# Four moves in the second half of a hand-ordered attention-and-MLP block

## The chip, the cores and the metric

One NeuronCore of a Trainium2 chip runs one program. The metric is its time on the device in microseconds (us), as the median of several executions. Five engines work side by side, each through its own queue in program order: TensorE (PE, matrix products), VectorE (DVE), ScalarE (ACT), GpSimd (POOL), and SyncE (SP), which here issues the transfers.

## The reference

The input x has 2048 rows of 576 numbers. Two branches are added to it: sliding-window attention on the layer-normed x, and a dense MLP with the Mish activation on the same layer-normed x.

```python
xn = _layernorm(x)
# A: 32 heads of 18; each position looks at itself and 7 earlier ones, 2 apart
qkv = xn @ wqkv
logits = einsum("bhsd,bhswd->bhsw", q, kg) * scale      # w = 8 window places
o = einsum("bhsw,bhswd->bhsd", softmax(logits), vg)
A = o @ wo                                              # 576 x 576
# B: 576 -> 4608 -> 576
h = xn @ w1 + b1
B = (h * tanh(softplus(h))) @ w2
return x + A + B
```

All of it is in 32-bit floats.

## The kernel before, in words

**Numbers.** Every matrix operand is kept as two tiles, a *high part* (the value rounded to the format that TensorE reads, written by ACT) and a *low part* (value minus high part, written by DVE or POOL). A product is three matmuls per 128 rows of depth: high x high, high x low, low x high. So `prod`, which multiplies two such rows of depth, issues six matmuls (L669), and `rest`, for the last 64 columns of the 576, two (L675).

**Halves, pairs, parts.** The 2048 rows are done in two halves (`hf` 0 and 1) of 1024. In each half the 4608 hidden columns are done in 18 *pairs* `q` of 2 x 128. For one pair, `m1_part` computes the first MLP product by a scheme with seven products in place of eight, on sums of quarter blocks (`S1`... from `Ss`, and the weight sums `t0`, `t1`), in six *parts*. They use three PSUM banks of the tag "h" (`cur[1]` to `cur[3]`): part 0 fills bank 1 and bank 2, part 2 goes on in bank 1, part 1 fills bank 3 ("the third product"), part 3 goes on in bank 1, part 4 in bank 3 and part 5 in bank 1. After parts 0, 2 and 3, `take` (L703, ACT) copies bank 1 to a tile (c11, c21, c22) before the next part goes on in the same bank. `mish` then adds a bank to such a copy (L714, DVE) and applies Mish (L715, ACT). For the first pair (q = 0) the six parts run in the order 0, 2, 1, 3, 5, 4, and two of the Mish steps are held back until part 5.

**Items.** In the second half the second MLP product of the first eight pairs is also done with seven products instead of eight. Two pairs make a group `e` (0 to 3), with seven *items* `k` (0 to 6), called item e.k here: `p_item` multiplies a left operand (24 matmuls into four "out" banks, L859) and adds the four results to accumulators (`accP`, DVE L865; for some of the first group copied by ACT, L863). Left operands are an activation quarter or a sum: `u_sum` (L801) makes the sums S1 to S4 in place, `u_high` (L807, ACT) the high part, `u_low` (L813, DVE or POOL) the low part, all for each of the group's two pairs `qq`. Items need S3, A22, A11, S1, A12, S2, S4 in this order; the sum S2 is made near item 0. `p_join` (L868, POOL) adds accumulators to each other at the end. Pairs 8 to 17 go the plain way: `m2_cols`, four *chunks* of 24 matmuls each (L880), added up by DVE (L883); `a_split` (L821 ACT, L822 POOL) makes the high and low parts of pair 8's activations, `mish` itself those of the later pairs (L720, L721).

**Attention.** `attention(hf)` is a generator, advanced one *step* at a time. A step first flushes the reduction of the step before (DVE, L538 or L577) and then puts two multiplications on POOL (L533 `pr` or L571 `pv`). Steps of the second half run in the slots listed in `cuts[1]`.

**Order.** All work stands in a list `plan` of *slots*. A slot has its own matmuls (with the evictions behind them) and a list of background functions, filled by `before(i, fn)`, which are issued ahead of the slot's own work. What a slot leaves behind (`pend`, `soon`) is issued in the next slot, around its background. A manual dependency holds each engine to this order, so an operation that waits holds up all behind it on its engine. Around the end of the items the slots are, in order: part 8.4, item 3.3, part 8.5, item 3.4, item 3.5, part 9.0, item 3.6, part 9.1, part 9.2, chunk (1,0), part 9.3, chunk (1,1), part 9.4, chunk (0,0), part 9.5, chunk (0,1), with part q.n for part n of pair q and the chunks being those of pair 8. In the slots from part 9.0 to part 9.1, POOL has in the background: two joins and a low half of `a_split`; two joins and two low halves, and then the low half of a Mish; two joins and a low half.

**The end.** After pair 17's four chunks (1,0), (1,1), (0,0), (0,1) come sixteen output products with `wo` in three parts each (`wo_part`, L1063, in "h" banks). Each needs its attention tile split and summed by `o_split`, in four steps 0 to 3 (DVE L914 and L917; L929 and L930; L935; L938 and L939). For the first output tile these steps use three "h" banks and run beside pair 17's chunks.

Of the kernel before, what the change touches and what calls it, by code (L numbers as in the profile page):

```python
# [17 lines left out]
P = 128  # L18
# [13 lines left out]
OC = 4  # L32
# [7 lines left out]
def block_kernel(ctx: ExitStack, tc: tile.TileContext, x, wq, wo, w1, b1, w2, mask, out):  # L40
    nc = tc.nc
# [617 lines left out]
    cur = {}  # L659
    late = []  # L660

    def bank(hf, q, n):
        cur[n] = ps.tile([P, TB], F32, tag="h", bufs=4, name=f"h{n}_{hf}_{q}")
        return cur[n]

    def prod(ph, wt, off, X, hi, lo, first, last):
        seq = [(off + k, wl, xs + k) for k in range(2) for wl, xs in ((0, hi), (0, lo), (1, hi))]
        for i, (wk, wl, xs) in enumerate(seq):
            nc.tensor.matmul(ph, wt[:, wl, wk * P:(wk + 1) * P], X[:, xs, :],  # L669
                             start=first and i == 0, stop=last and i == len(seq) - 1,  # L670
                             skip_group_check=True)

    def rest(ph, wt, off, X, xs):
        for wl in range(2):
# [52 lines left out]
    def m1_part(hf, q, part):  # L727
        X0, X1 = XTs[hf, 0], XTs[hf, 1]
        if part == 5 and late:
            for fn in late[::-1]:  # L730
                fn()
            late.clear()
        wa, wc, t0, t1 = (done.get((k, hf, q)) for k in ("wa", "wc", "t0", "t1"))
        if part == 0:
            prod(bank(hf, q, 1), wa, 0, X0, 0, 5, True, True)
            take(hf, q, "c11")
            prod(bank(hf, q, 2), wa, 2, X0, 2, 7, True, False)
            rest(cur[2], wa, 4, X0, 4)
            mish(hf, q, 0, 0, cur[2], cur["c11"])
        elif part == 1:  # L740
            prod(bank(hf, q, 3), t1, 0, X1, 0, 5, True, True)
        elif part == 2:
            prod(cur[1], t0, 2, Ss[hf, 1], 0, 2, False, True)
            take(hf, q, "c21")
        elif part == 3:
            prod(cur[1], t0, 0, Ss[hf, 0], 0, 2, False, False)
            rest(cur[1], wc, 2, X1, 4)
            take(hf, q, "c22")
        elif part == 4:
            prod(cur[3], t1, 2, X1, 2, 7, False, False)  # L750
            rest(cur[3], wa, 4, X1, 4)
            mish(hf, q, 1, 0, cur[3], cur["c21"])
        else:
            prod(cur[1], wc, 0, Ss[hf, 2], 0, 2, False, False)
            rest(cur[1], wc, 2, X1, 9)
            mish(hf, q, 0, 1, cur[1])
        if part == 3:
            mish(hf, q, 1, 1, cur[3], cur["c22"])
# [383 lines left out]
    plan = []  # L1142
    at = {}
    US = {"q": 2.75, "z": 2.5, "p": 3.15, "t": 0.6, "o": 2.6}
    PART = (3.2, 1.4, 1.4, 1.8, 1.8, 1.8)

    def add(tag, *fns, alias=None):
        at[tag] = at[alias] = len(plan)
# [2 lines left out]
    def before(i, fn):  # L1151
        plan[max(i, 0)][1].append(fn)

    def qi(hf, g, b, jj, alias=None):
        add(("q", hf, g, b, jj), lambda: qkv_item(hf, g, b, jj), alias=alias)

    def zi(jj, part):
        add(("z", jj, part), lambda: z_part(1, jj, part))

    def mi(hf, q, part, alias=None):  # L1160
        add(("m", hf, q, part), lambda: m1_part(hf, q, part), alias=alias)
# [68 lines left out]
    def quad(hf, q):  # L1230
        if q == 0:
            for part, ids in ((0, (0,)), (2, (1, 2)), (1, (3, 4)), (3, (5, 6)), (5, (7, 8)), (4, (9,))):
                for p_ in {}.get(part, ()) if hf else ():
                    zi(JB - 1, p_)
                if part == 5 and hf == 0:
                    qi(hf, NQ - 1, 0, JB - 1)
                mi(hf, 0, part)
                for i in ids:
                    at["s", hf, 0, i] = len(plan) - 1
            return  # L1240
        if hf and q <= 2 * OC + 1:
            C9 = list(((1,0),(1,1),(0,0),(0,1)))
            if q == 1:
                seq = ((0, (0,)), (2, (1, 2)), (1, (3, 4)), (3, (5, 6)), (4, (7, 8)), (5, (9,)))
            elif q == 2 * OC:
                seq = ((0, (0,)), (1, (1,)), ("N", (2,)), (2, (3,)), ("N", (4,)), (3, (5,)), ("N", (6,)), (4, (7,)), ("N", (8,)),
                                (5, (9,)), ("N", ()))
            elif q == 2 * OC + 1:
                seq = (("N", (0,)), (0, ()), ("N", (1,)), (1, ()), (2, (2,)), ("C", (3,)), (3, (4,)), ("C", (5,)), (4, (6,)), ("C", (7,)), (5, (8,)), ("C", (9,)))
            elif q % 2 == 0:  # L1250
                seq = (0, 1, "N", 2, "N", 3, "N", 4, "N", 5) if q > 2 else (0, 2, "N", 1, "N", 3, "N", 4, "N", 5)
                seq = [(p_, (i,)) for i, p_ in enumerate(seq)]
            else:
                seq = [(p_, (i, 9)[0:1 + (i == 8)]) for i, p_ in enumerate((0, 1, 2, "N", 3, "N", 4, "N", 5))]
            for part, ids in seq:
                if part == "N":
                    pi()
                elif part == "C":
                    pr_(1, q - 1, *C9.pop(0))
                else:  # L1260
                    for p_ in {4:(3,)}.get(part, ()) if q == 1 else ():
                        zi(JB - 1, p_)
                    mi(1, q, part)
                for i in ids:
                    at["s", 1, q, i] = len(plan) - 1
            return
        k = 0
        late_chunks = q == 1 or (hf, q) == (1, NP - 1)
        for i, part in enumerate((0, 1, 2, None, 3, None, 4, None, 5, None) if late_chunks else
                                 (0, 1, None, 2, None, 3, None, 4, None, 5)):  # L1270
            if (hf, q) == (0, NP - 1) and i in (5, 7, 9):
                tr(0, (i - 5) // 2)
            alias = ("s", hf, q, i)
            if part is not None:
                mi(hf, q, part, alias)
            else:
                pr_(hf, q - 1, *CHUNKS[k], alias)
                k += 1
# [65 lines left out]
    for q in range(NP):  # L1344
        if q == 0:
            i = at["q", 0, 3, 1, 0]
            ps_ = dict(raw=i - 3, sums=i - 1, wa=i, wc=i + 1, t0=i + 2, t1=i + 4)
        elif q == 1:
            i = at["q", 0, 3, 0, 0]
# [16 lines left out]
    for q in range(1, 2 * OC + 1):  # L1366
        i = spot(0, q, (3,2)[q > 1])
# [5 lines left out]
    i = spot(0, NP - 1, 0)  # L1373
# [5 lines left out]
    i = at["q", 1, 0, 1, 1]  # L1379
# [4 lines left out]
    i = spot(0, 9, 4)  # L1384
# [10 lines left out]
    for q in range(NP):  # L1395
        if q == 0:
            i = at["z", JB - 1, 0]
            ps_ = dict(wa=i - 7, t0=i - 6, t1=i - 5, wc=i - 4)
        elif q == 1:
            i = spot(1, 0, 0)  # L1400
# [9 lines left out]
    for g, (e, k, s) in enumerate(items):  # L1410
        lead = items[g - 3][2] if g >= 3 else spot(1, 0, 5) + 2 * g
        before(lead + 1, lambda e=e, k=k: p_fetch(e, k))
        for qq in range(2):
            ds = {(0, 0): (-6, -5, -5), (0, 1): (-2, -1, 0), (1, 0): (0, -4, -2), (1, 1): (0, -2, -2), (2, 0): (0, -3, -2), (2, 1): (0, -3, -2), (3, 0): (-4, -3, -2), (3, 1): (-4, -2, -1), (4, 0): (0, -3, -3), (4, 1): (0, -3, -2), (5, 0): (-1, -3, -3), (5, 1): (0, -3, -2), (6, 0): (-4, -3, -1), (6, 1): (-4, -3, -2)}[k, qq]
            for d, f in zip(ds[1:], (u_high, u_low)):
                before(s + d, lambda f=f, e=e, k=k, qq=qq: f(e, k, qq))
            s2 = items[7 * e + (0 if k == 5 else k)][2] + ds[0]
            before(s2, lambda e=e, k=k, qq=qq: u_sum(e, k, qq))
    J = 2 * OC + 1
    for n, (a, b) in enumerate((("P6", "P1"), ("P7", "P6"), ("P6", "P5"), ("P2", "P1"), ("P3", "P6"), ("P4", "P7"), ("P5", "P7"))):  # L1420
        for pr in range(2):
            i = items[-2][2] + 1 + (0,1,2)[n] if n < 3 else at["p", 1, J + 0 - 1, n > 4, pr] + (1, 7, 1, 2)[n - 3]
# [6 lines left out]
    i = at["q", 0, 1, 1, 0]  # L1429
# [3 lines left out]
    i = at["q", 0, 3, 1, 0]  # L1433
# [5 lines left out]
    i = at["q", 1, 0, 1, 1]  # L1439
    for n in range(8):  # L1440
        c, k = divmod(n, 4)
# [7 lines left out]
    for n in range(0, JB, 2):  # L1449
        i = at["q", 0, 1, 0, n]  # L1450
# [4 lines left out]
    for n in range(TJ):  # L1455
        i = spot(0, 2 + n, 2)
# [3 lines left out]
    i = spot(0, NP - 2, 0)  # L1460
# [7 lines left out]
    for n, (name, pr) in enumerate((name, pr) for name in ("P4", "P5", "P2", "P3") for pr in range(2)):  # L1468
        i = items[dict(P4=0, P5=2, P3=2, P2=3)[name]][2] + pr
# [23 lines left out]
    cuts = [[], []]  # L1493
    k = marks[0] - 1
    for n in range(steps - len(last_steps)):
        t = 6.111 * n
        k = next(k for k in range(k + 1, len(plan)) if T[k + 1] > t and ok[k])
        cuts[0].append(k)
    cuts[0] += last_steps
    early = {0: (8,), 1: (0, 2, 4, 6, 8), 2: (0, 3, 6), 3: (0, 3, 6), 4: (0, 4, 7), 5: (0, 3, 7), 6: (1, 4, 7),  # L1500
             7: (0, 4, 7), 8: (1, 4, 8), 9: (1, 3, 7)}
    for q in range(NP):
        cuts[1] += [spot(1, q, i) for i in early.get(q, (1, 3, 5, 7, 9))]
        if q == 2 * OC:
            cuts[1].append(at["p", "x", OC - 1, 4])
    cuts[1] = sorted(set(cuts[1])) + [at["p", 1, NP - 1, *c] for c in CHUNKS]
    cuts[1] = cuts[1][:steps]
    assert len(cuts[0]) == len(cuts[1]) == steps, (len(cuts[0]), len(cuts[1]), steps)
# [5 lines left out]
    i = spot(1, *(11,3))  # L1514
# [4 lines left out]
    for n, name in enumerate(("T3", "T1", "T2", "T4", "B11", "B21", "B22", "R", "D")):  # L1519
        k = i + 10 + (2, 5, 10, 15, 20, 25, 30, 35, 40)[n]  # L1520
# [5 lines left out]
    i = spot(1, NP - 1, 0)  # L1526
# [3 lines left out]
    j = at["p", 1, NP - 1, 1, 0]  # L1530
# [4 lines left out]
        before(j + -1, lambda k=k: o_load(0, k))  # L1535
        before(j + 1, lambda k=k: o_load(0, 2 + k))
    for k in range(4):
        before(j + (1, 1, 2, 3)[k], lambda k=k: o_split(0, k, True))
    for p_ in range(TJ // 2):
        before((j + 1, at["o", 0, 0], at["o", 0, 2], at["o", 1, 2])[p_], lambda p_=p_: y_load(p_))  # L1540
    for k in range(4, 2 * TJ):
# [8 lines left out]
    last = {}  # L1550
# [44 lines left out]
```

## Time and profile before

| what | value |
|---|---|
| median of 3 runs | 1114.05 us (1113.94 to 1114.44) |
| the profiled execution | 1114.25 us, span 1112.5 us |
| PE busy | 1101.6 us, 99% |
| DVE busy | 849.5 us, 76% |
| POOL busy | 790.8 us, 71% |
| ACT busy | 499.5 us, 45% |
| granted TensorE clock | 1.000 |

The span runs from the first to the last instruction of the profile; the time on the device is 1.75 us longer in that execution. In a row of the timeline the first number is the start, the second the duration, then engine, line, operation, result <- operands, shape and count; a bracket gives the idle time of that engine before it and what ended it.

### The profile page before, as it was taken

Reading aid. Unit: us, or ns where it says so; the run is one execution under the profiler, and the core shown is the slowest. Engines: PE = TensorE matmul, PEld = TensorE weight load, DVE = VectorE, ACT = ScalarE, POOL = GpSimd, SP = SyncE. Lnnn points to the kernel's source line nnn. Section 1 sums busy time; section 2 is a strip of 40 time slices with the busy share of each in tenths; the row PEclk is TensorE's granted clock in tenths of the full one; section 3 lists DMA queues with packets and bytes.
Section 4 is the critical chain, followed back from the end, with each engine's and each line's share of the span. In section 5 each row is a group of like instructions: output and inputs, shape, how many; then the busy total and the mean of one; then the engine's idle time right before and its main releaser. Section 6 shows DMA issues by size and latency. Waiting matters only on the chain.

```text
span 1112.5 us, 18203 instructions
## 1 busy us (share of the span) xinstructions
PE 1101.6 (99%) x6550; PEld 1015.2 (91%) x6550; DVE 849.5 (76%) x1367; ACT 499.5 (45%) x917; POOL 790.8 (71%) x639
## 2 busy tenths in 40 slices
PE   9999999999999999999999999999999999999998
PEld 8999899999999999999999889989989999999998
DVE  6369788888889888897656577786776677777786
ACT  5544655544454544555333354433433344343353
POOL 2479777766679688785788676666688976867532
PEclk9999999999999999999999999999999999999999
DMA  6899696868777758675597898565664657776574
GB/s 202 283 312 316 225 356 214 285 233 276 258 242 264 268 208 301 249 249 204 190 323 241 245 375 307 211 196 196 220 222 170 209 195 223 244 288 219 171 232 142
DMA packets 178270, 271.60 MB, mean 244 GB/s; under 512 B 53218, under 2 KB 120068, under 8 KB 178180
## 3 DMA queue, kind: packets, MB, share of 16 engines
q1 hardware_dynamic: 178180, 270.44, 71.6%
q8 instruction: 52, 0.85, 0.3%
q14 instruction: 38, 0.31, 0.1%
HBM read 160.39 MB, written 110.00 MB: 243 GB/s over the span
## 4 chain that ended last, share of the span: by engine, by line
PE 87%; POOL 6%; DVE 3%; issue 2%; ACT 1%; DMA 0%; SPq 0%; POOLq 0%; DVEq 0%; ACTq 0%
PE h L669 28%; PE po L767 21%; PE pq L348 9%; PE po L880 9%; PE po L859 6%; PE h L675 5%; PE o L1063 5%; PE z L446 3%; POOL pv L571 2%; POOL accP L868 1%; POOL pr L533 1%; POOL act L721 1%; POOL s L620 1%; DMA acc<-in_x 0%; PE ta L75 0%
## 5 line engine op out<-in xcount | busy, mean ns | idle before, releaser
L767 PEld LDWEIGHTS po<-w,act 128*128 128x128 f32 x1728 | 236.4, 188 | 6.0 <-POOL act L721 0.4
L767 PE MATMUL po<-w,act 128*128 128x288 f32 x1728 | 240.7, 295 | 0.1
L533 POOL TENSOR_TENSOR pr<-q,kv 128x576 f32<-128x576 f32 x128 | 196.9, 1563 | 8.5 <-DMA q<-q_d 5.0
L721 POOL TENSOR_TENSOR act<-c,act 128x512 fp32r<-128x512 f32 x81 | 107.3, 1325 | 128.6 <-ACT act L720 128.6
L571 POOL TENSOR_TENSOR pv<-L,kv 128x576 f32<-128x576 f32 x128 | 177.9, 1484 | 26.1 <-DVE L L564 21.2
L771 DVE TENSOR_TENSOR acc<-po,acc 128x288 f32<-128x288 f32 x288 | 119.4, 448 | 29.9 <-PE po L767 29.0
L348 PE MATMUL pq<-wq,xt 128*128 128x432 f32 x672 | 136.5, 361 | 1.0 <-ACT xt L81 1.0
L880 PEld LDWEIGHTS po<-w,act 128*128 128x128 f32 x960 | 130.9, 188 | 4.6 <-DVE accP L883 1.8
L880 PE MATMUL po<-w,act 128*128 128x288 f32 x960 | 133.5, 295 | 1.0 <-DVE accP L883 1.0
L348 PEld LDWEIGHTS pq<-wq,xt 128*128 128x128 f32 x672 | 125.0, 188 | 8.0 <-ACT xt L81 1.8
L715 ACT ACTIVATE c<-c,b1c 128x512 f32<-128x512 f32 x81 | 58.7, 725 | 140.7 <-DVE c L714 140.4
L669 PE MATMUL h<-xt,t 128*128 128x512 f32 x432 | 110.6, 391 | 0.5 <-DVE rt L714 0.3
L669 PE MATMUL h<-S,t 128*128 128x512 f32 x432 | 110.5, 391 | 0.0
L577 DVE TENSOR_REDUCE og<-pv 128x144 f32<-128x1152 f32 x64 | 86.0, 1345 | 25.7 <-POOL pv L571 25.6
L669 PE MATMUL h<-xt,wa 128*128 128x512 f32 x432 | 104.1, 390 | 0.0
L538 DVE TENSOR_REDUCE L<-pr 128x64 f32<-128x1152 f32 x64 | 85.8, 1341 | 23.8 <-POOL pr L533 23.7
L703 ACT COPY c<-h 128x512 f32<-128x512 f32 x81 | 47.4, 586 | 124.1 <-PE h L675 73.0
L859 PEld LDWEIGHTS po<-pw,u 128*128 128x128 f32 x672 | 92.2, 188 | 5.4 <-DVE u L813 2.1
L859 PE MATMUL po<-pw,u 128*128 128x288 f32 x672 | 94.3, 295 | 2.5 <-DVE u L813 1.6
L669 PEld LDWEIGHTS h<-xt,wa 128*128 128x128 f32 x432 | 80.9, 188 | 17.0
L669 PEld LDWEIGHTS h<-xt,t 128*128 128x128 f32 x432 | 79.0, 188 | 15.7 <-DVE rt L714 0.7
L883 DVE TENSOR_TENSOR accP<-po,accP 128x288 f32<-128x288 f32 x160 | 68.9, 452 | 29.8 <-PE po L880 28.2
(228 smaller groups left out, 1853.8 us busy)
## 6 DMA issues: line engine op xcount, KB each, us to landing
kv<-kv_d SPq DMA_DIRECT2D x64, 396.0 KB, 5.1
kept_t<-t SPq DMA_DIRECT2D x36, 512.0 KB, 4.8
t<-kept_t SPq DMA_DIRECT2D x36, 512.0 KB, 6.7
rw<-in_w SPq DMA_DIRECT2D x36, 320.0 KB, 4.4
kept_wa<-wa SPq DMA_DIRECT2D x18, 640.0 KB, 4.7
kept_w<-w SPq DMA_DIRECT2D x20, 576.0 KB, 4.1
wa<-kept_wa SPq DMA_DIRECT2D x18, 640.0 KB, 5.2
w<-kept_w SPq DMA_DIRECT2D x20, 576.0 KB, 4.1
```

What stands on the lines that cost most here:

```text
L348: nc.tensor.matmul(pq[:, 0:432], XT[:, xi, tok], wt[wi][:, hl, 0:432], start=i == 0, stop=i == len(seq) - 1)
L533: nc.gpsimd.tensor_tensor(out=pr[:, x:x + hh], in0=q[:, j0 + x:j0 + x + hh, None, :].to_broadcast([P, hh, W, CU]), in1=win(kt, 0, CU, j0 + ...
L538: nc.vector.tensor_reduce(L[:, k, j0:j0 + hj].rearrange("p j w h -> p (j w h)"), pr.rearrange("p j w (h d) -> p (j w h) d", h=2), axis=AX, ...
L571: nc.gpsimd.tensor_tensor(out=pr[:, x:x + hj].rearrange("p j d w -> p j w d"), in0=L[:, k, x:x + hj, :, h:h + 1].to_broadcast([P, hj, W, DH]),
L577: nc.vector.tensor_reduce(og[:, c0:c0 + DH, :].rearrange("p d j -> p j d"), pr, axis=AX, op=ALU.add)
L669: nc.tensor.matmul(ph, wt[:, wl, wk * P:(wk + 1) * P], X[:, xs, :], start=first and i == 0, stop=last and i == len(seq) - 1, skip_group_ch ...
L721: nc.gpsimd.tensor_tensor(out=a[:, 1, :], in0=t, in1=a[:, 0, :].bitcast(F32), op=ALU.subtract)
L767: nc.tensor.matmul(po, acts[hf, q, b, j][:, al, tok], done["w2", hf, 2 * q + j][:, wl, c * HC:(c + 1) * HC], start=i == 0, stop=i == 5)
L771: nc.vector.tensor_tensor(out=t, in0=po, in1=t, op=ALU.add)
L859: nc.tensor.matmul(po, units[e, k, qq][:, al, tok], w[:, qq, wl, :], start=i == 0, stop=i == 5)
L880: nc.tensor.matmul(po, acts[hf, q, b, j][:, al, tok], done["w2", hf, 2 * q + j][:, wl, c * HC:(c + 1) * HC], start=i == 0, stop=i == 5)
L883: nc.vector.tensor_tensor(out=t, in0=po, in1=t, op=ALU.add)
```

## The change

- **Third product of the first pair.** `prod` can issue a subset of its six matmuls. In the second half, part 1 of pair 0 issues three of them, and a new part 6, a slot of its own between parts 3 and 5, the other three. All later slots move on by one in the list; places that are given relative to them stay with them.
- **One low part.** The low part of S3 for item 0.0, pair 1 (`u_low(0, 0, 1)`, DVE), is issued in the background of the slot ahead of the item, right behind its high part, and no longer in the item's own slot. In that slot, the sum S2 for pair 0 stands behind it now, and so does the addition L714 of pair 2's first Mish.
- **Attention steps.** The step in item 3.4's slot goes to part 9.0's; those in the slots of item 3.6 and chunk (1,0) go to parts 9.2 and 9.3. The one in chunk (0,0) stays.
- **First output tile.** The four steps of `o_split(0, ...)` were in the background of chunks (1,1), (1,1), (0,0), (0,1) of pair 17; they now follow the matmuls and additions of chunks (1,1), (0,0), (0,0), (0,1).

```diff
-    def prod(ph, wt, off, X, hi, lo, first, last):
+    def prod(ph, wt, off, X, hi, lo, first, last, some=range(6)):
         seq = [(off + k, wl, xs + k) for k in range(2) for wl, xs in ((0, hi), (0, lo), (1, hi))]
         for i, (wk, wl, xs) in enumerate(seq):
-            nc.tensor.matmul(ph, wt[:, wl, wk * P:(wk + 1) * P], X[:, xs, :],
-                             start=first and i == 0, stop=last and i == len(seq) - 1,
-                             skip_group_check=True)
+            if i in some:
+                nc.tensor.matmul(ph, wt[:, wl, wk * P:(wk + 1) * P], X[:, xs, :],
+                                 start=first and i == 0, stop=last and i == len(seq) - 1,
+                                 skip_group_check=True)
...
         elif part == 1:
-            prod(bank(hf, q, 3), t1, 0, X1, 0, 5, True, True)
+            prod(bank(hf, q, 3), t1, 0, X1, 0, 5, True, True, range(3) if (hf, q) == (1, 0) else range(6))
+        elif part == 6:
+            prod(cur[3], t1, 0, X1, 0, 5, True, True, range(3, 6))
...
-    PART = (3.2, 1.4, 1.4, 1.8, 1.8, 1.8)
+    PART = (3.2, 1.4, 1.4, 1.8, 1.8, 1.8, 0.7)
...
                 if part == 5 and hf == 0:
                     qi(hf, NQ - 1, 0, JB - 1)
+                elif part == 5:
+                    mi(hf, 0, 6)
                 mi(hf, 0, part)
...
+            if (e, k, qq) == (0, 0, 1):
+                ds = (-2, -1, -1)
             for d, f in zip(ds[1:], (u_high, u_low)):
...
-             7: (0, 4, 7), 8: (1, 4, 8), 9: (1, 3, 7)}
+             7: (0, 4, 7), 8: (1, 4, 8), 9: (2, 4, 7)}
...
         if q == 2 * OC:
-            cuts[1].append(at["p", "x", OC - 1, 4])
+            cuts[1].append(at["m", 1, 2 * OC + 1, 0])
...
     for k in range(4):
-        before(j + (1, 1, 2, 3)[k], lambda k=k: o_split(0, k, True))
+        plan[j + (1, 2, 2, 3)[k]][0].append(lambda k=k: o_split(0, k, True))
```

`PART` feeds a planner's clock for the first half only; the new slot lies behind all that it places.

## The prediction

> **What bounds the kernel now.** I read the page first, then TensorE's waits, the chain of waits, and the timeline of each engine around the four places that the diff touches.
>
> ```profile
> PE 1101.6 (99%) x6550; PEld 1015.2 (91%) x6550; DVE 849.5 (76%) x1367; ACT 499.5 (45%) x917; POOL 790.8 (71%) x639
> ...
> PE po L859 <- DVE u L813: 1.6, 1, 1.6
> ...
> PE po L880 <- DVE accP L883: 1.0, 1, 1.0
> PE po L859 <- ACT u L807: 0.8, 1, 0.8
> ...
> 881.75 3.18 PE po L880 x24
> ```
>
> TensorE is busy for 99% of the span of 1112.5 us, so the change can only win gaps. These three waits and a fourth of 0.68 us (its row stands in the next part) are all of any size in the second half, 4.1 us together, and each lies at one of the edits. The last line, from the chain, is the price of one item or chunk: 24 matmuls in 3.18 us, 0.1325 us each. The profiled execution took 1114.25 us, 0.20 above the median of 1114.05. I sum differences in its timeline and add them to the median.
>
> **Third product in two runs.** PE, then ACT:
>
> ```profile
> 629.46 1.52 PE L669 MATMUL h<-xt,t 128*128 128x512 f32 x6
> 630.82 1.53 PE L669 MATMUL h<-S,t 128*128 128x512 f32 x6
> 632.19 0.63 PE L675 MATMUL h<-xt,wc 128*128 128x512 f32 x2
> 633.49 1.66 PE L669 MATMUL h<-S,wc 128*128 128x512 f32 x6 [0.68 <-ACT rt L703]
> ...
> 629.71 0.59 ACT L703 COPY rm<-h 128x512 f32<-128x512 f32 x1 [2.65 <-PE h L669]
> 632.86 0.58 ACT L703 COPY rt<-h 128x512 f32<-128x512 f32 x1 [2.56 <-PE h L675]
> ```
>
> A matmul of this width takes (630.82 - 629.46) / 6 = 0.227 us. Part 3 has issued its last at 632.19 + 0.45 = 632.64, and part 5 begins at 633.49, because it overwrites the bank that ACT copies until 633.44: 0.85 us lost (the row counts from the modelled end). The three matmuls that now stand there fill 0.68 and leave 0.17. They are taken from behind part 2, whose copy ends at 630.30: part 3 could begin at 629.46 + 0.68 = 630.14 and waits until 630.34, 0.20 lost. Net 0.85 - 0.17 - 0.20: **0.5 us gained** (ends 0.85 and 0). The addition of bank 3 to c22 now waits for part 6, which ends before 633.49 as well; part 4, which goes on in that bank, comes behind part 5. The new slot moves some loads past one slot on SP's queue; I cost that at nothing, since they are issued several parts ahead. If that cover were gone, an item would start late by a part, 1.36 us.
>
> **The low part one slot earlier.** DVE, PE and POOL:
>
> ```profile
> 653.93 1.61 DVE L801 TENSOR_TENSOR rm<-rt,rm 128x512 f32<-128x512 f32 x1
> 655.46 0.68 DVE L714 TENSOR_TENSOR ra<-h,ra 128x512 f32<-128x512 f32 x1
> 656.06 1.16 DVE L813 TENSOR_TENSOR u<-rm,u 128x512 fp32r<-128x512 f32 x1
> ...
> 654.88 0.82 PE L859 MATMUL po<-pw,u 128*128 128x288 f32 x5
> 657.27 2.78 PE L859 MATMUL po<-pw,u 128*128 128x288 f32 x19 [1.57 <-DVE u L813]
> ...
> 654.96 1.71 POOL L813 TENSOR_TENSOR u<-rt,u 128x512 fp32r<-128x512 f32 x1
> ...
> 657.96 1.30 POOL L813 TENSOR_TENSOR u<-rt,u 128x512 fp32r<-128x512 f32 x1 [1.30 <-ACT u L807]
> ...
> 662.90 1.76 DVE L801 TENSOR_TENSOR ra<-ra,rm 128x512 f32<-128x512 f32 x1 [3.70 <-POOL u L813]
> 664.59 1.54 DVE L865 TENSOR_TENSOR accP<-po,accP 128x288 f32<-128x288 f32 x4
> ...
> 666.27 0.97 PE L859 MATMUL po<-pw,u 128*128 128x288 f32 x6
> ```
>
> Item 0.0 issues five matmuls and waits for the low part, third of these DVE rows. Moved up, it takes the first place, starts at 653.93 and is ready by about 655.54, when the sixth matmul (654.88 + 0.66) wants it: 657.27 - 655.54 = 1.7 us gained there. What is now late: the sum S2 and the addition for pair 2's mish. The addition starts at 656.5 instead of 655.46 if the two swapped rows keep their joint duration, and at 657.2 if S2 has to wait out the POOL row of 654.96 (ends 656.67) as the low part did. Behind it on ACT queue the mish, a copy and item 0.1's high part, then on POOL its low part (657.96 now), an attention pair, the low parts of item 0.2, and behind the first of these on DVE the row at 662.90, in front of the four additions that free item 0.1's banks. All of that moves by 1.1 to 1.7. The first bank, now free at 664.59 + 0.46 = 665.05, is free at 666.1 to 666.8, and item 0.2, which could have begun 1.7 us before 666.27, begins there. So the gain is given back two items later: -0.1 to +0.5, I take **0.3 us lost**, nearer the POOL row, because the low part next to that row behaved so.
>
> The Trainium skill (SBUF — State Buffer, "Who interferes with whom") says that a VectorE instruction with two SBUF inputs contends with a GpSimd instruction that reads SBUF, and that the one that issues first blocks the other. By that the later start, 657.2, would hold, and the term would be +0.5; by the joint duration it would be -0.1. The low part's end at 657.22, 0.55 us behind POOL's, agrees.
>
> **Attention steps.** PE, DVE, POOL from item 3.4 on, and one PE row farther on:
>
> ```profile
> 812.61 3.38 PE L859 MATMUL po<-pw,u 128*128 128x288 f32 x24
> 816.82 3.41 PE L859 MATMUL po<-pw,u 128*128 128x288 f32 x24 [0.82 <-ACT u L807]
> ...
> 829.14 3.41 PE L880 MATMUL po<-w,act 128*128 128x288 f32 x24
> ...
> 837.57 1.55 PE L669 MATMUL h<-xt,t 128*128 128x512 f32 x6
> ...
> 813.17 1.92 DVE L801 TENSOR_TENSOR rm<-rm,ra_r 128x512 f32<-128x512 f32 x1
> ...
> 816.27 1.54 DVE L865 TENSOR_TENSOR accP<-po,accP 128x288 f32<-128x288 f32 x4
> ...
> 832.51 1.35 DVE L538 TENSOR_REDUCE L<-pr 128x64 f32<-128x1152 f32 x1 [5.43 <-POOL pr L533]
> ...
> 835.88 0.68 DVE L714 TENSOR_TENSOR c<-h,c 128x512 f32<-128x512 f32 x1
> ...
> 812.63 3.73 POOL L533 TENSOR_TENSOR pr<-q,kv 128x576 f32<-128x576 f32 x2
> 819.87 3.29 POOL L868 TENSOR_TENSOR accP<-accP,accP 128x576 f32<-128x576 f32 x2 [3.51 <-DVE accP L865]
> ...
> 824.38 2.81 POOL L868 TENSOR_TENSOR accP<-accP,accP 128x576 f32<-128x576 f32 x2
> ...
> 829.66 2.81 POOL L533 TENSOR_TENSOR pr<-q,kv 128x576 f32<-128x576 f32 x2
> ...
> 865.54 1.63 PE L669 MATMUL h<-xt,t 128*128 128x512 f32 x6 [0.24 <-DVE c L714]
> ```
>
> Item 3.5 could begin at 812.61 + 3.18 = 815.79 and begins at 816.82. The row names ACT, but the first of DVE's additions for item 3.4 ends at 816.27 + 0.46 = 816.73, late because the sum of 813.17 runs beside POOL's pair and a reduction follows. Without the step there, that wait goes: 1.03 gained.
>
> But POOL is the tighter queue afterwards. It used the idle time from 812.63 for the pair of multiplications, and its rows from 824.38 on show no idle time before them. Now the pair stands in part 9.0's slot, behind the first joins. Those need two results of item 3.5 added up: 815.79 + 12 x 0.1325, the end of a matmul and two additions, about 818.2. Then in queue order two joins (2.8), a split's low half (1.3, as the POOL row of 657.96), the pair (2.8), two joins (2.8), two low halves (2.6): 830.5. The chunk that needs the last of them began at 829.14 and would now at 828.1; its sixth matmul waits from 828.8 to 830.5, 1.7 us. It ends at 833.0; part 9.3 (8 x 0.227) and the second chunk bring TensorE to part 9.4 at 838.0. Part 9.4 overwrites a bank that DVE adds from (835.88 now), and that addition is queued behind the reduction of the next attention pair. This reduction waits for POOL: 830.5, a low half (1.3), two joins (2.8), a low half (1.3), the pair (2.8), so 838.7. Then 1.35 and 0.68: part 9.4 begins at 840.75 instead of 837.57, **3.2 us later**. Of that, 0.3 comes back before 865.54, where TensorE now waits for a chain through POOL, which is later by only about 1.1. So **2.9 us lost**. Ends: 1.3 gained (both waits gone, POOL in time) and 3.7 lost (DVE's two-input work slipping in between POOL's, as it did in 3.29 against 2.81).
>
> **First output tile.** DVE and PE:
>
> ```profile
> 1047.06 0.41 DVE L914 TENSOR_TENSOR s<-ot,o 128x256 f32<-128x256 f32 x1
> ...
> 1048.38 1.54 DVE L883 TENSOR_TENSOR accP<-po,accP 128x288 f32<-128x288 f32 x4
> ...
> 1053.19 0.43 DVE L939 TENSOR_TENSOR ob<-ot,ob 64x256 fp32r<-64x256 f32 x1
> ...
> 1048.88 6.63 PE L880 MATMUL po<-w,act 128*128 128x288 f32 x48 [1.01 <-DVE accP L883]
> 1055.35 1.75 PE L1063 MATMUL o<-wo,oa 128*128 128x288 f32 x12
> ```
>
> Four operations of steps 0 and 1 (1048.38 - 1047.06 = 1.32) stand ahead of the additions whose first frees the bank for 1048.88. Behind them, that bank is free at 1047.06 + 0.46, before TensorE wants it: 1.1 gained, and the output starts at about 1054.25. Now step 3 is late: the last addition ends near 1054.9, and its two DVE operations at 1055.35 and 1055.8. The output's second product, due after six matmuls at 1055.05, needs the bank of step 3's operand: it waits 0.3 (bank freed by the first) to 0.8 (by the second). **0.5 us gained** (ends 1.1 and 0).
>
> **Sum.** -0.5 + 0.3 + 2.9 - 0.5 = +2.2: 1116.3 us.
>
> **Rivals.** *All four gaps close.* POOL and DVE keep pace: -0.5 - 1.7 - 1.3 - 1.1 = -4.6, 1109.5 us; with half of the attention's and the low part's gain, -3.1, 1111.0. For it: the edits sit at the four waits. Against: POOL is without a gap behind 819.87, so work put there must come out. It decides itself by whether the second pair of attention multiplications ends before 836, which is 838.0 less the reduction and the addition.
>
> *POOL is late, but TensorE meets it only at the end.* The attention term is then POOL's own delay, 2.8 for the pair less 1.7 for the earlier joins, 1.1; net +0.4, 1114.5 us. Against: the reduction stands ahead of the addition in DVE's queue.
>
> *DVE is shut out for longer.*
>
> ```profile
> 851.98 3.68 DVE L554 TENSOR_TENSOR L<-L,m 128x256 f32<-128x256 f32 x1
> ```
>
> Here a DVE operation on half of L801's columns took 3.68 us, some 2 us beyond L801's. Should that meet item 3.6's low part, now beside unbroken POOL work from 818.2 on, TensorE waits those 2 us more: +4.2, 1118.3 us. The Trainium skill's same section allows it; only this row shows it so long.
>
> **How the numbers follow.** Forecast 55%, its own range +0.9 (-0.6 - 0.1 + 2.4 - 0.8) to +3.5 (-0.4 + 0.5 + 3.7 - 0.3); all gaps close 25%; POOL at the end only 8%; shut out 12%. About 0.2% (2.2 us) is what a measurement of this kernel can tell from no change; the forecast lies on that bound, with rather more room above: 30 of its 55 go to slower, 25 to same. Faster 0.25; same 0.25 + 0.08 = 0.33; slower 0.30 + 0.12 = 0.42. The range, 1111.0 to 1118.3, leaves out the lower half of the first rival and the upper half of the last, 18%.
>
> **What would show it.** Right: the waits of 1.57, 0.82, 0.68 and 1.01 are gone; item 0.2 waits for DVE's L865 additions; the first chunk waits near 829 for POOL act L822, part 9.4 for DVE c L714 by over 2 us; the output's second product waits for DVE L938 or L939. Wrong: no wait of TensorE between 825 and 845 means that the attention term is a gain, and no wait at item 0.2 that the low part's gain stays.

## The result and the profile after

The changed kernel takes 1116.22 us (median of 12 executions, 1116.03 to 1118.55) against 1114.30 (12 executions, 1113.77 to 1115.05): ratio 1.0020, 95% interval 1.0011 to 1.0028, so 1.2 to 3.1 us slower. The medians differ by 1.9. The forecast was 1116.3.

The profiled execution after took 1118.55 us with a span of 1116.7. It is 2.3 us above its own median. A drop of TensorE's clock, shown below, lengthens some of its rows by 1.6 us. I therefore read from it where waits come and go, and not its total.

TensorE's largest waits after, from the view of waits (engine, tile, line <- engine, tile, line waited for: us in total, times, longest; "issue" stands where the profile shows no releaser):

```profile
PE h L670 <- DVE c L715: 2.2, 1, 2.2
PE po L883 <- POOL act L825: 2.0, 1, 2.0
...
PE po L862 <- issue: 1.2, 1, 1.2
```

The lines of the program behind the first edit moved by one to three: L670 was L669, L676 was L675, L715 was L714, L804 was L801, L810 was L807, L816 was L813, L825 was L822, L862 was L859, L868 was L865, L871 was L868, L883 was L880, L942 was L939, L1066 was L1063, L1070 was L1067. The four waits of before, 4.1 us together, are gone. Three new ones, 5.4 us together, stand in their place, and the two largest are in the stretch that the attention steps were moved into.

**Ahead of item 0.2.** TensorE's timeline before and after, from the last part that the change doesn't touch, and then DVE's and one row of POOL's after:

```profile
624.88 2.93 PE L669 MATMUL h<-xt,wa 128*128 128x512 f32 x12
```

```profile
625.19 2.93 PE L670 MATMUL h<-xt,wa 128*128 128x512 f32 x12
...
629.77 0.84 PE L670 MATMUL h<-xt,t 128*128 128x512 f32 x3
630.66 1.66 PE L670 MATMUL h<-S,t 128*128 128x512 f32 x6
632.15 0.64 PE L676 MATMUL h<-xt,wc 128*128 128x512 f32 x2
632.63 0.86 PE L670 MATMUL h<-xt,t 128*128 128x512 f32 x3
633.47 1.67 PE L670 MATMUL h<-S,wc 128*128 128x512 f32 x6
...
654.83 3.54 PE L862 MATMUL po<-pw,u 128*128 128x288 f32 x24
...
666.78 3.44 PE L862 MATMUL po<-pw,u 128*128 128x288 f32 x24 [1.17 <-issue]
```

```profile
653.90 1.61 DVE L816 TENSOR_TENSOR u<-rm,u 128x512 fp32r<-128x512 f32 x1
655.43 1.77 DVE L804 TENSOR_TENSOR rm<-rt,rm 128x512 f32<-128x512 f32 x1
657.12 0.68 DVE L715 TENSOR_TENSOR ra<-h,ra 128x512 f32<-128x512 f32 x1
...
666.23 1.54 DVE L868 TENSOR_TENSOR accP<-po,accP 128x288 f32<-128x288 f32 x4
```

```profile
654.92 1.73 POOL L816 TENSOR_TENSOR u<-rt,u 128x512 fp32r<-128x512 f32 x1
```

This execution was already 0.31 us late ahead of the first edit (625.19 against 624.88). The third product's two runs are the rows with x3; the stretch up to part 5 shrinks from 633.49 - 624.88 = 8.61 to 633.47 - 625.19 = 8.28. Item 0.0 now runs without a gap, and the wait reappears at item 0.2, which starts at 666.78, behind the first of the four additions (666.23 + 0.46 = 666.69).

**Behind item 3.4.** TensorE, POOL and DVE after:

```profile
813.19 6.55 PE L862 MATMUL po<-pw,u 128*128 128x288 f32 x48
...
831.44 2.79 PE L883 MATMUL po<-w,act 128*128 128x288 f32 x19 [1.96 <-POOL act L825]
...
841.46 2.80 PE L670 MATMUL h<-xt,t 128*128 128x512 f32 x6 [2.22 <-DVE c L715]
...
844.91 3.41 PE L883 MATMUL po<-w,act 128*128 128x288 f32 x24
...
870.50 1.55 PE L670 MATMUL h<-xt,t 128*128 128x512 f32 x6
```

```profile
818.80 3.31 POOL L871 TENSOR_TENSOR accP<-accP,accP 128x576 f32<-128x576 f32 x2 [5.53 <-DVE accP L868]
...
830.11 1.28 POOL L825 TENSOR_TENSOR act<-rt,act 128x512 fp32r<-128x512 f32 x1
...
836.59 2.84 POOL L533 TENSOR_TENSOR pr<-q,kv 128x576 f32<-128x576 f32 x2
```

```profile
839.46 1.35 DVE L538 TENSOR_REDUCE L<-pr 128x64 f32<-128x1152 f32 x1 [4.58 <-POOL pr L533]
840.73 0.68 DVE L715 TENSOR_TENSOR c<-h,c 128x512 f32<-128x512 f32 x1
```

Items 3.4 and 3.5 are one row of 48 matmuls now, so the gap of 0.82 is closed. POOL stood idle for 5.53 us instead, and its chain of joins, attention multiplications and low halves has the third low half (L825) ready at 831.39; chunk (1,0) resumes at 831.44. The second pair of multiplications ends at 839.43. The reduction starts at 839.46, the addition behind it ends at 841.41, and part 9.4 starts at 841.46. Relative to before (837.57) that is 3.89 later, of which 0.58 is the lateness item 3.4 already had (813.19 against 812.61).

The view by windows shows the drop of the clock in this execution (the window's length; busy us and instructions of PE, PEld, DVE, ACT and POOL; then the granted clock, DMA share, GB/s):

```profile
841.00:846.00 5.00, 4.54 (x16) 3.77 (x17) 3.94 (x8) 1.47 (x3) 5.00 (x4) 0.66 0.00 0
```

From 841 to 846 TensorE's granted clock was 0.66; in the five microseconds before and behind that it was 1.00. Part 9.4's eight matmuls last from 841.46 to 844.91, 3.45 us, where eight at the forecast's 0.227 take 1.8: some 1.6 us on top of the wait.

**The first output tile.** TensorE before and after, and DVE's last operation of step 3 after:

```profile
1038.18 9.69 PE L880 MATMUL po<-w,act 128*128 128x288 f32 x72
...
1057.21 1.75 PE L1063 MATMUL o<-wo,oS 128*128 128x288 f32 x12
```

```profile
1043.05 16.06 PE L883 MATMUL po<-w,act 128*128 128x288 f32 x120
1058.95 1.76 PE L1066 MATMUL o<-wo,oa 128*128 128x288 f32 x12
1060.73 0.53 PE L1066 MATMUL o<-wo_r,ob 128*128 128x288 f32 x2
1061.22 1.86 PE L1066 MATMUL o<-wo,oS 128*128 128x288 f32 x12
```

```profile
1060.25 0.43 DVE L942 TENSOR_TENSOR ob<-ot,ob 64x256 fp32r<-64x256 f32 x1
```

The five chunks up to the output are one row without a gap. The two matmuls that read `ob`, the last of the output's first part, have to wait for L942, which ends at 1060.68. The second part (the row with `oS`) then starts 0.49 behind them, where it was 1057.21 - 1056.94 = 0.27 before: its weight load waited 0.19 us for an addition (L1070) that stands behind L942 on DVE.

### The profile page after: what moved, and what is told of

It reads as the page before. It is cut to its first block, busy times and chain, and to the rows that moved or that the text cites. A ratio compares the mean times of both kernels' runs of the same rounds, so it can differ in the third digit from the quotient of the medians.

```text
span 1116.7 us, 18204 instructions
## 1 busy us (share of the span) xinstructions
PE 1103.3 (99%) x6550; PEld 1015.4 (91%) x6550; DVE 847.3 (76%) x1367; ACT 499.4 (45%) x917; POOL 790.2 (71%) x639
## 4 chain that ended last, share of the span: by engine, by line
PE 89%; POOL 4%; DVE 2%; issue 1%; DMA 1%; ACT 1%; DVEq 0%; POOLq 0%; SPq 0%
PE h L670 28%; PE po L770 20%; PE po L883 11%; PE pq L348 9%; PE po L862 7%; PE h L676 5%; PE o L1066 5%; PE z L446 3%; POOL pv L571 1%; DMA acc<-in_x 1%; POOL s L620 1%; POOL act L722 1%; POOL pr L533 0%; DVE rm L804 0%; PE ta L75 0%
## 5 line engine op out<-in xcount | busy, mean ns | idle before, releaser
L883 PEld LDWEIGHTS po<-w,act 128*128 128x128 f32 x960 | 131.2, 188 | 5.2 <-POOL act L825 2.2
L883 PE MATMUL po<-w,act 128*128 128x288 f32 x960 | 133.2, 295 | 2.0 <-POOL act L825 2.0
L670 PE MATMUL h<-xt,t 128*128 128x512 f32 x432 | 111.9, 394 | 2.5 <-DVE c L715 2.2
L670 PE MATMUL h<-S,t 128*128 128x512 f32 x432 | 110.5, 391 | 0.0
L670 PE MATMUL h<-xt,wa 128*128 128x512 f32 x432 | 104.1, 390 | 0.0
L862 PEld LDWEIGHTS po<-pw,u 128*128 128x128 f32 x672 | 92.1, 188 | 5.1 <-issue 1.6
L670 PEld LDWEIGHTS h<-xt,wa 128*128 128x128 f32 x432 | 80.9, 188 | 17.0
L670 PEld LDWEIGHTS h<-xt,t 128*128 128x128 f32 x432 | 79.7, 189 | 17.9 <-DVE c L715 2.5
L862 PE MATMUL po<-pw,u 128*128 128x288 f32 x672 | 94.4, 296 | 1.6 <-issue 1.2
```

Source lines behind the costliest of these rows:

```text
L862: nc.tensor.matmul(po, units[e, k, qq][:, al, tok], w[:, qq, wl, :], start=i == 0, stop=i == 5)
L883: nc.tensor.matmul(po, acts[hf, q, b, j][:, al, tok], done["w2", hf, 2 * q + j][:, wl, c * HC:(c + 1) * HC], start=i == 0, stop=i == 5)
```

## The experiments

**The theories.** Mine, from the prediction: each wait moves to the next operation behind it, and the slowdown is the attention steps, through POOL's queue (at chunk (1,0)) and the reduction ahead of the addition on DVE (at part 9.4). The rivals: the three other edits cost something too; or the attention steps are harmless and the loss is something else, such as DVE held out by POOL, or the drop of the clock alone. Every ratio below is to the kernel before, executed on the same chip; of two medians, the second is that of the kernel before.

**The attention steps alone, and everything but them.** `d_only` is the kernel before with these lines:

```diff
-             7: (0, 4, 7), 8: (1, 4, 8), 9: (1, 3, 7)}
+             7: (0, 4, 7), 8: (1, 4, 8), 9: (2, 4, 7)}
...
-            cuts[1].append(at["p", "x", OC - 1, 4])
+            cuts[1].append(at["m", 1, 2 * OC + 1, 0])
```

`no_d` is the changed kernel with the same lines put back.

> Only the attention steps are moved. Theory (POOL's queue order is what costs): +2.7 to +3.5 us against before, more than the whole change, with TensorE waiting 1.7 to 2.1 us for POOL act L822 in chunk (1,0) and 2.1 to 2.7 us for DVE c L714 at part 9.4, and no wait at item 3.5. Rival (the loss comes from the other edits, the attention steps only move a gap): within 0.5 us of before.

> The change with the attention steps put back to their old slots (items 3.4 and 3.6, chunk (1,0)). Theory (terms add up: -0.3 for the third product, +0.5 for the low part, -0.7 for the output tile): -0.5 us against before, 2.5 us faster than the whole change, and no slow matmuls behind part 9.4. Rival (the low part's lag reaches the later items): slower than before by 1 us or more.

`d_only`: 1118.09 against 1114.40, ratio 1.0032 (1.0019 to 1.0045), of only five executions. `no_d`: 1113.91 against 1114.40, 0.9998 (0.9989 to 1.0007). TensorE's waits of `d_only`, its window of the low clock, and the row of item 3.5 in `no_d`:

```profile
PE h L669 <- DVE c L714: 2.5, 2, 2.2
PE po L880 <- POOL act L822: 2.0, 1, 2.0
```

```profile
841.00:846.00 5.00, 5.00 (x21) 4.27 (x22) 3.73 (x7) 1.86 (x3) 5.00 (x5) 0.67 0.00 0
```

```profile
817.06 3.40 PE L862 MATMUL po<-pw,u 128*128 128x288 f32 x24 [0.85 <-ACT u L810]
```

The steps alone bring both new waits and the low clock, and cost 3.7 us between the medians, a little above the expected range; without them both are absent and the old wait at item 3.5 is back, with 0.85. This settles the first point: the loss is the attention steps, and the other three edits together cost nothing that can be measured.

**The first step alone, the later two alone.** Each is one of the two hunks of `d_only`: `d_first` the second (item 3.4's step to part 9.0), `d_second` the first (item 3.6's and chunk (1,0)'s steps to parts 9.2 and 9.3).

> Of the attention steps only the first is moved, from item 3.4's slot to part 9.0's; the later two stay. Theory: POOL still has the pair of multiplications ahead of the low halves, so chunk (1,0) waits 1.9 to 2.1 us for POOL act L822, but the second pair follows at once, so part 9.4 waits under 0.3 us for DVE's addition; net +0.9 to +1.3 us. Rival (the two later steps cost nothing of their own): +2.9 or more, as with all three.

> Of the attention steps only the later two are moved (to parts 9.2 and 9.3); the first stays at item 3.4. Theory (the later steps have a price of their own: their multiplications stand behind the joins and low halves of part 9.1's slot, and DVE's reduction waits for them ahead of the addition that part 9.4 needs): no wait in chunk (1,0), a wait of 1.8 to 2.5 us for DVE c L714 at part 9.4, +1.9 to +2.4 us. Rival (only the first step's place costs): within 0.4 us of before.

`d_first`: 1115.67 against 1114.69, 1.0010 (1.0001 to 1.0019). `d_second`: 1116.41 against 1114.45, 1.0022 (1.0013 to 1.0031). TensorE's timeline of the one and of the other:

```profile
831.00 2.79 PE L880 MATMUL po<-w,act 128*128 128x288 f32 x19 [1.96 <-POOL act L822]
...
838.79 1.55 PE L669 MATMUL h<-xt,t 128*128 128x512 f32 x6
```

```profile
839.44 1.63 PE L669 MATMUL h<-xt,t 128*128 128x512 f32 x6 [2.19 <-DVE c L714]
```

The two losses are separate. The first step's place costs the wait for POOL at chunk (1,0), less the gap won at item 3.5: about 1 us. The later two steps' place costs the wait at part 9.4, about 2 us, although no wait stands at chunk (1,0) there. Their sum, 3, is near the forecast's 2.9. Some executions of both had the low clock; the medians of those at full clock, listed below, lie 0.7 and 1.6 us above before. In the timelines, counted from item 3.4 to part 10.4 (865.54 before), the two cost 1.23 and 1.62 us.

**The first step one slot later only.** `d_alt` puts it into item 3.5's slot, where POOL is still idle:

```diff
-            cuts[1].append(at["p", "x", OC - 1, 4])
+            cuts[1].append(at["p", "x", OC - 1, 5])
```

> The first attention step is moved one slot only, from item 3.4's to item 3.5's, the later two stay. POOL's multiplications then keep the idle time that they use in the kernel before, and only DVE's reduction moves behind item 3.4's additions. Theory: the wait of 0.82 us at item 3.5 goes and POOL's chain behind it starts about 0.7 us earlier: -0.5 to -0.9 us. Rival (any later place for this step costs POOL): +0.5 or more.

1114.12 against 1114.69, 0.9997 (0.9988 to 1.0005): by its time alone nothing is decided. TensorE's timeline:

```profile
812.68 6.55 PE L859 MATMUL po<-pw,u 128*128 128x288 f32 x48
...
829.42 2.79 PE L880 MATMUL po<-w,act 128*128 128x288 f32 x19 [0.45 <-POOL act L822]
```

The gap ahead of item 3.5 is gone here too, and the wait at chunk (1,0) is 0.45 instead of 1.96. So what costs in the change, for this step, is the length of the move, past POOL's idle time, and not the move itself. For the later two steps no shorter move was run.

**Is the clock's drop the loss?** `d_fill` is `d_only` with eight matmuls ahead of part 9.4, whose result nothing reads, so that TensorE isn't idle in the second wait:

```diff
+            if (hf, q) == (1, 2 * OC + 1):
+                fill = ps.tile([P, TB], F32, tag="h", bufs=4, name="fill")
+                for i in range(8):
+                    nc.tensor.matmul(fill, t1[:, 0, 0:P], X1[:, 0, :], start=i == 0, stop=i == 7, skip_group_check=True)
             prod(cur[3], t1, 2, X1, 2, 7, False, False)
```

> All three attention steps are moved, and 8 matmuls (128x512, into a bank that nothing reads) stand ahead of part 9.4, in the time in which TensorE waited. Theory (the slow matmuls behind part 9.4, granted clock 0.67 there, come from the two waits of 2 us close to each other): the clock stays at 1.00 between 841 and 846, the time is +2.8 to +3.3 us against before, with no runs above +4. Rival (the clock falls for another reason): clock again near 0.67, runs up to +5.

1117.80 against 1114.69, 1.0025 (1.0015 to 1.0035). In its profiled execution, which took 1116.62, the clock stayed up:

```profile
841.00:846.00 5.00, 5.00 (x34) 4.66 (x33) 4.12 (x9) 2.12 (x4) 5.00 (x5) 1.00 0.00 0
```

The loss stays 2.8 us by the ratio (1.7 to 3.9), and 1.9 us in an execution at full clock (1116.62 against the median 1114.69). The five executions of the changed kernel at full clock agree: their median of 1116.16 is 1.9 us above the 1114.30 of before. So the waits are the loss, and the clock can add to it. The rest must be read over all executions, each of which has a mean granted clock; five microseconds at 0.66 lower it to 0.998. Executions below 1.000, and the median time at 1.000 and below it:

```
d_only     5 of 5            -        1118.09
after      7 of 12     1116.16        1116.41
d_fill     5 of 8      1116.66        1118.10
d_first    5 of 11     1115.41        1116.13
d_second   4 of 11     1116.03        1117.67
d_alt      0 of 11     1114.12              -
best       0 of 11     1113.42              -
no_d, c_only, e_only, c_sum_later   6 of 44
before     3 of 78
```

A drop thus goes with TensorE waits of about 2 us, in some executions and not in all. By the medians, those executions are 0.3 to 1.6 us longer. In the changed kernel it is only 0.3: five of its seven took 1116.13 to 1116.55, so the drop does not by itself explain the 1118.55 of the profiled one. The filling did not keep it away in general: the first wait, 1.97 us, was still there. That idleness is the cause was not shown by a run that removes both waits and leaves the rest of the order alone.

**The low part alone, and with S2 later.** `c_only` is the kernel before with the hunk of the low part. `c_sum_later` adds that S2 for pair 0 goes to the item's own slot, behind the addition instead of ahead of it:

```diff
+            if e == 0 and k in (0, 5):
+                ds = {(0, 0): (-6, -5, -5), (0, 1): (-2, -1, -1), (5, 0): (0, -3, -3), (5, 1): (0, -3, -2)}[k, qq]
```

> Only the low part of S3 is issued one slot earlier. Theory (the gap moves two items on, since the sum S2 and the addition L714 are now behind it): +0.3 to +0.6 us, item 0.0 without a wait over 0.1 us, item 0.1 waiting about 0.8 in two places, item 0.2 about 1.2. Rival (the gap closes): -1.7 us and item 0.2 begins 1.7 us earlier than before.

> The low part of S3 one slot earlier, and the sum S2 for pair 0, which then stood behind it and ahead of the addition L714, moved to the item's own slot, behind that addition. Theory (the low part alone would win; what gives it back is the sum and the addition that it pushed behind itself): -0.9 to -1.3 us against before, item 0.2 waiting some 0.6 us at most. Rival (the gap moves on whatever stands behind the low part): +0.3 to +0.6 us, as with the low part alone.

`c_only`: 1114.94 against 1114.40, 1.0002 (0.9993 to 1.0011). `c_sum_later`: 1114.37 against 1114.69, 0.9998 (0.9989 to 1.0006). Neither time tells them from no change; the timelines do. In `c_only`, item 0.0 starts at 654.83 and item 0.2 at 666.78, as in after. TensorE in `c_sum_later`:

```profile
655.14 3.51 PE L859 MATMUL po<-pw,u 128*128 128x288 f32 x24
...
665.44 3.41 PE L859 MATMUL po<-pw,u 128*128 128x288 f32 x24 [0.42 <-issue]
...
818.03 4.96 PE L859 MATMUL po<-pw,u 128*128 128x288 f32 x24 [2.41 <-ACT rm L715]
```

From item 0.0 to item 0.2 it was 666.27 - 654.88 = 11.39 before, is 666.78 - 654.83 = 11.95 in `c_only`, and 665.44 - 655.14 = 10.30 with S2 behind the addition. So it is S2 ahead of the addition, and the chain from there to item 0.2, that turned a gain of 1.1 into a loss of 0.56.

The last of these rows is a surprise at a place that this edit doesn't touch: item 3.5 waited 2.41 us. The row names ACT, but the first of DVE's additions ahead of it ended at 817.49 + 0.46 = 817.95. DVE and POOL in the same execution, and the window behind it:

```profile
811.24 4.46 DVE L813 TENSOR_TENSOR u<-ra_r,u 128x512 fp32r<-128x512 f32 x1 [0.20 <-ACT u L807]
...
817.49 1.53 DVE L865 TENSOR_TENSOR accP<-po,accP 128x288 f32<-128x288 f32 x4
```

```profile
811.04 1.35 POOL L801 TENSOR_TENSOR ra<-ra,rm 128x512 f32<-128x512 f32 x1
812.29 2.86 POOL L533 TENSOR_TENSOR pr<-q,kv 128x576 f32<-128x576 f32 x2
```

```profile
818.00:823.00 5.00, 4.96 (x25) 5.00 (x26) 3.57 (x8) 0.00 (x0) 1.41 (x1) 0.66 0.33 132
```

The first of these DVE operations ended 0.55 us behind the last of three POOL operations in a row, the row of one and the row of two. The same operation in the kernel before, on DVE's timeline, was let in behind the first of the same three (its POOL row of 812.63 is the pair):

```profile
811.60 1.64 DVE L813 TENSOR_TENSOR u<-ra_r,u 128x512 fp32r<-128x512 f32 x1 [0.20 <-ACT u L807]
```

The order of these operations is the same in both kernels, and POOL's first one starts 0.2 us ahead of DVE's in both, so the edit does not explain it. There is one trace for each kernel; eight of the twelve kernels have these three POOL operations there, and in the other seven it took 1.64 to 1.67 us. Why this one differs stays open.

**The output tile's steps alone.** `e_only` is the kernel before with that hunk.

> Only the first output tile's steps stand behind the additions. Theory: the wait of 1.0 us ahead of chunk (0,0) goes and the second output product waits 0.3 to 0.6 us for step 3's DVE operations, net -0.5 to -0.9 us. Rival (step 3 holds up two products): 0.

1113.79 against 1114.40, 0.9995 (0.9986 to 1.0004). In its own timeline it is 1056.50 - 1038.34 = 18.16 us from the start of the five chunks to the output's second part, where it was 1057.21 - 1038.18 = 19.03; in after it is 1061.22 - 1043.05 = 18.17. The gain of 0.87 shows whole in the timeline and is too small for the times to settle.

**What the runs point to.** `best` keeps the third product's two runs, takes S2 later from `c_sum_later`, the first attention step from `d_alt` with the other two back in their old slots, and puts step 3 of the output tile one chunk earlier:

```diff
-        plan[j + (1, 2, 2, 3)[k]][0].append(lambda k=k: o_split(0, k, True))
+        plan[j + (1, 2, 2, 2)[k]][0].append(lambda k=k: o_split(0, k, True))
```

> All four places, each with the cause taken out: the third product in two runs; the low part earlier and the sum S2 for pair 0 behind the addition; the first attention step one slot later only, the others kept; the output tile's steps 0 to 2 as changed, step 3 behind chunk (0,0)'s additions too, not (0,1)'s. Theory: -0.3 - 1.1 - 0.3 - 1.2 = -2.9 us against before, the output's second product without a wait. Rival (POOL's chain or the output's operands take back the half): -1.5 or less of a gain.

1113.42 against 1114.45, ratio 0.9989 (0.9980 to 0.9998): faster than the kernel before, by 1.0 us between the medians where 2.9 was expected. The expectation's rival, a gain of 1.5 or less, came true. TensorE's timeline of its profiled execution (1112.26 us, span 1110.5, the fastest of eleven up to 1115.07), and one line of its waits:

```profile
664.48 3.45 PE L862 MATMUL po<-pw,u 128*128 128x288 f32 x24 [0.40 <-issue]
...
828.55 2.79 PE L883 MATMUL po<-w,act 128*128 128x288 f32 x19 [0.46 <-POOL act L825]
...
1055.14 1.86 PE L1066 MATMUL o<-wo,oS 128*128 128x288 f32 x12 [0.25 <-DVE y L1070]
```

```profile
PE po L862 <- DVE accP L868: 0.6, 1, 0.6
```

Three rests of the old waits remain, 1.1 us together: item 0.2, chunk (1,0), and the output's second part. The last line is a new wait of 0.59 us, ahead of item 0.5, where the kernel before had none (`c_sum_later` has 0.21 there): part of a wait moved on once more. The gain in this execution is 2.0 us of span. What makes the other executions up to 2.8 us longer was not profiled; their clock was 1.000. The hold-out of DVE seen above is a candidate and no more.

## Why the prediction was right, step by step

**The sum** was +2.2 and the ratio gives +2.2 (1.2 to 3.1). Its size is the attention term, as forecast. The profiled execution adds to that the 0.31 by which it was late ahead of the first edit, and the 1.6 of the clock: its span is 4.2 longer, and 4.2 - 0.3 - 1.6 = 2.3. That the sum is so close is partly luck: the four terms measure -0.33, +0.56, some +2.8 and -0.86, so they were off by about +0.2, +0.3, -0.1 and -0.4, and these cancel.

**The attention steps** (forecast +2.9) came out row by row. Taking off the 0.58 by which this execution was late: the joins started at 818.22 (818.2 forecast), the third low half was ready at 830.81 (830.5), part 9.4 started at 840.88 (840.75). The waits were 1.96 (1.7) and 2.22. The later start of part 9.4 is 3.31 (3.2), and `d_first` plus `d_second` give 3.0 by the times. The small excess is the first two joins, 3.31 where I had put 2.8. By the row of 870.50 (865.54 before) it is 4.38 later, which is 3.31 and the clock's 1.6 less some 0.5 that came back, where I had put 0.3. Without the clock's 1.6 that is 2.8, and `d_fill`, at full clock, gives the same by its own row. Not forecast was the clock: I priced a wait of TensorE at its length alone.

**The low part** (forecast +0.3, ends -0.1 and +0.5) was mis-sized: +0.56, in after and in `c_only`, just above the upper end. The step that failed is the choice between the two ends. I had the addition at 656.5 or 657.2 and took a value between. It started at 657.12, because S2, at 655.43, lasted 1.77 us and ended 0.55 behind the POOL row of 654.92. The additions that free item 0.2's banks began 1.64 later (666.23 against 664.59 before), where I had 1.1 to 1.7. By the Trainium skill (SBUF — State Buffer, "Who interferes with whom"), the engine that issues first blocks the other, which was the upper end: the trace agrees with it, at 657.12 against 657.2.

**The third product** (forecast -0.5) gave -0.33; `no_d` and `best` show the same stretch of 8.28. The waits that I predicted, 0.20 and 0.17, are there: 630.66 - 629.77 - 0.68 = 0.21 and 633.47 - 632.63 - 0.68 = 0.16. What I left out is that matmuls behind a gap took longer: part 3 takes 632.15 - 630.66 = 1.49, where it took 632.19 - 630.82 = 1.37 without a gap ahead of it. The split makes two such restarts out of one, 0.12 more. It was not run by itself; the differences of the medians, `no_d` less `c_only` less `e_only`, -0.49 - 0.54 + 0.61, give -0.4.

**The output tile** (forecast -0.5) gave -0.86: the gap of 1.01 closed and 1.27 was won up to the output's start (1043.05 to 1058.95 is 15.90, and 1038.18 to 1055.35 was 17.17); 0.41 was given back up to the second part (1061.22 - 1058.95 = 2.27 instead of 1.86). The step that failed is that the output's second product would wait, from its first matmul, for the bank of step 3's operand. Its first six matmuls did not wait. Its last two did, for L942's result, and the second part did, for the addition that stands behind L942. `e_only` gives the same 2.27.

**The rivals.** That all gaps close fell with the waits at chunk (1,0) and part 9.4: the second pair of multiplications ended at 839.43, where it would have had to end by 836. That POOL's lateness is met only at the end fell too, with `d_second`. That DVE is shut out for longer did not happen in the profiled execution of after. In `c_sum_later` it did, in another place, ahead of item 3.5.

## What to carry to other kernels

In an order written by hand, price a moved operation at what the next waits on its new engine queue become, not at the wait that it leaves: here 4.1 us of waits went and 5.4 came. Look first which idle time of its queue the work used in its old place, and whether the new place lies behind it; here a move of one slot, ahead of the end of POOL's idle time, closed the same gap as the move of two, past it. And a wait of TensorE of 2 us may cost more than its length, so it is worth checking the granted clock in the windows behind it.

## What the runs showed of the hardware

**The clock dropped behind short waits.** The granted clock was 0.66 to 0.67 in the five microseconds behind waits of 1.96 and 2.22 us with 7.8 us of work between them (after; `d_only` has nearly the same), and behind a single one of 2.41 (`c_sum_later`). Behind the two waits, the eight matmuls of part 9.4 lasted 3.45 us in after and 844.36 - 840.83 = 3.53 in `d_only`, where they took 839.42 - 837.57 = 1.85 before. With one wait of 2 us it was 1.00 in the profiled executions of `d_first` and `d_second`, and below 1.000 on the mean in 9 of their 22 executions. The Trainium skill (TensorE: Matmul & The Clock Gate, "HAM oscillation — how this bites in real kernels") warns of idle gaps above some 3.4 us; here the drops stood behind gaps shorter than that, and the measurement decides. Its section "What's actually happening" says that the window in which activity is counted runs freely. That would fit with a drop in some executions and not in others; no run here shows the window, nor that the gaps caused the drops.

**One DVE operation, three durations.** The low part u of 128x512 with two inputs in SBUF took 1.64 us and 4.46 us at the same place of the order, and 1.16 to 1.61 at item 0.0. Against three POOL operations in a row it got in behind the first or, in one of eight traces with the same order there, only behind the last (4.46).
